# Reordering the first transfers, statistics and transposes at the head of a fused layer-norm, SwiGLU and attention kernel

## The chip, the cores and the metric

One core of one Trainium2 chip. The metric is the device time of one execution in microseconds (us). The kernel before takes 921.5 us. The change touches only the first 13 us.

## The reference

Everything is bf16. x has 2048 tokens (rows) of 640 values. It is layer-normed. The normed rows feed two branches: 32 heads of attention over a cached window of 512 keys, and a SwiGLU feed-forward with 1536 hidden units. The output is x plus the product of both.

```python
xn = _layernorm(x, axis=-1)                       # (x - mean) / sqrt(var + 1e-5)
s = _A_ref(xn, A_k_cache, A_v_cache, A_wq, A_wo)  # windowed attention, then @ wo
g = _silu((_silu(xn @ w_gate) * (xn @ w_up)) @ w_down)
return x + s * g
```

## The kernel before

It begins with the feed-forward of the first 512 tokens, as four token tiles of 128 rows. For each tile: load x, statistics on VectorE (two halves and an aggregation), square root on ScalarE, reciprocal and apply on VectorE, five transposes on TensorE (with 128 x 128 pieces), copies back to SBUF, and then 30 matmuls of 128 columns with the first quarters of the gate and up weights. Each quarter's load is cut in two: a first piece (rows 0 to 255, 192 KB) and a rest (rows 256 to 639, 288 KB). In the traces TensorE, VectorE and ScalarE each start their instructions in the order of the calls, even where a later one could run: in order_alone below, VectorE idles 1.65 us ahead of one call while the data of the next is there. So the place of a call in this code is its place in the queue.

```python
        load_x(0, (nc.scalar, nc.sync))         # half of tile 0 from each queue
        load_x(1, (nc.scalar,))
        load_first(slice(0, 2))                 # first gate piece, first up piece: SyncE's queue
        load_first(slice(2, NC), (nc.sync, nc.scalar))   # gate rest: SyncE, up rest: ScalarE
        nc.scalar.activation(act_t[:], one_t[:], ACT.Sqrt)   # loads the table early
        load_x(2)
        load_x(3)
        load_gu(1)
        # ... further loads
        keep_warm(9)                            # dummy matmuls of 512 columns
        keep_warm(6, P)                         # and of 128 columns

        def ln_stats(t, between=None):
            # ...
            for g in range(ng):                 # ng = 2 halves
                nc.vector.bn_stats(stats[:, g, :], x_t[t][:, g * (D // ng) : (g + 1) * (D // ng)])
                if g == 0 and between:
                    between()
            nc.vector.bn_aggr(ln[b][0][:, ti, :], stats[:])

        def ready(t):                           # transposes, then copies to xnT
            # ... five nc.tensor.transpose into two PSUM tiles
            for tp, cs in zip(tps, PARTS):
                part = tp[:, 0 : cs.stop - cs.start, :]
                if t == 3 and cs.stop == NC:
                    nc.vector.tensor_copy(out=xnT[:, cs, rows], in_=part)
                else:
                    nc.scalar.copy(xnT[:, cs, rows], part)

        ln_stats(0)
        ln_sqrt(0)
        ln_stats(1, lambda: ln_apply(0, (slice(0, 2 * P), slice(2 * P, D))))
        ready(0)
        ln_sqrt(1)
        # ... tile 0: 12 matmuls of the first pieces, then 9 of the gate rest, 9 of the up rest
            for k, (f, s, cs) in enumerate(order):
                if k == len(order) * 4 // 5 and t < 3:
                    if t == 1:
                        ln_stats(3, lambda: ln_apply(2))
                    else:
                        ln_apply(t + 1)
                    ready(t + 1)
                    if t == 0:
                        ln_stats(2)
                    if t < 2:
                        ln_sqrt(t + 2)
                    else:
                        nc.scalar.activation(act_t[:], one_t[:], ACT.Silu)
                hidden_mm(first[f][s][:, rows], s, f, rows, cs)
```

The softmax here doesn't subtract the row's maximum and nothing guards it: scores larger than these inputs give would overflow.

## Time and profile before

| | before |
|---|---|
| time, median of 3 runs | 921.5 us (920.9 to 921.61) |
| span in the profiled run | 919.0 us |
| TensorE busy | 912.8 us (99%) |
| first matmul on real data | 6.26 us |
| token tiles 1, 2, 3 start at | 8.82, 10.89, 12.96 us |

The timelines below have, in this order: start and duration in us, engine, source line, operation, what is written from what, shapes, count; in square brackets the engine's idle time before and what ended it. The transfer lines have size in KB and us from issue to landing.

### The profile page before, as it was taken

Reading aid. Unit: us, or ns where it says so; the run is one execution under the profiler, and the core shown is the slowest. Engines: PE = TensorE matmul, PEld = TensorE weight load, DVE = VectorE, ACT = ScalarE, POOL = GpSimd, SP = SyncE. Lnnn points to the kernel's source line nnn. Section 1 sums busy time; section 2 is a strip of 40 time slices with the busy share of each in tenths; the row PEclk is TensorE's granted clock in tenths of the full one; section 3 lists DMA queues with packets and bytes.
Section 4 is the critical chain, followed back from the end, with each engine's and each line's share of the span. In section 5 each row is a group of like instructions: output and inputs, shape, how many; then the busy total and the mean of one; then the engine's idle time right before and its main releaser. Section 6 shows DMA issues by size and latency. Waiting matters only on the chain.

```text
span 919.0 us, 23151 instructions
## 1 busy us (share of the span) xinstructions
PE 912.8 (99%) x9898; PEld 548.4 (60%) x9920; DVE 601.6 (65%) x844; ACT 474.4 (52%) x840; POOL 85.5 (9%) x269
## 2 busy tenths in 40 slices
PE   9999999999999999999999999999999999999998
PEld 5444444465757575756565656566666666665565
DVE  6443421467677777777777777676867777777657
ACT  4222222557464646565656565655555555556471
POOL 0000000000000000000000000000000000002976
PEclk9999999999999999999999999999999999999999
DMA  9312430045353534253534343435343444343525
GB/s 306 73 35 64 92 81 1 1 75 112 54 113 50 112 49 109 53 108 54 108 58 109 57 109 55 108 52 96 69 84 76 89 78 80 86 71 102 121 58 166
DMA packets 248166, 77.53 MB, mean 84 GB/s; under 512 B 228992, under 2 KB 248064, under 8 KB 248064
## 3 DMA queue, kind: packets, MB, share of 16 engines
q1 hardware_dynamic: 245712, 73.46, 38.6%
q10 hardware_dynamic: 2352, 2.61, 0.8%
q8 instruction: 77, 1.26, 0.6%
q14 instruction: 25, 0.20, 0.1%
HBM read 38.93 MB, written 2.62 MB: 45 GB/s over the span
## 4 chain that ended last, share of the span: by engine, by line
PE 99%; DMA 1%; SPq 0%; issue 0%; DVE 0%
PE mm L450 22%; PE sc L464 18%; PE mm L489 16%; PE sc L604 15%; PE sc L282 11%; PE mm L312 6%; PE sc L574 4%; PE sc L566 2%; PE mm L541 2%; PE mm L566 1%; DMA wg_sb<-in_B_w_gate_dram 1%; PE gu L282 0%; PE mm L321 0%; PE sc L541 0%; PE sc L489 0%
## 5 line engine op out<-in xcount | busy, mean ns | idle before, releaser
L468 ACT ACTIVATE p_t<-sc 128x1024 bf16<-128x1024 f32 x254 | 253.0, 1023 | 120.3 <-PE sc L464 120.3
L455 DVE TENSOR_REDUCE qT<-mm 128x512 bf16<-128x1024 f32 x189 | 231.1, 1223 | 99.1 <-PE mm L450 96.6
L519 ACT ACTIVATE O_b<-mm,r 128x192 bf16<-128x192 f32 x486 | 165.0, 422 | 183.3 <-issue 139.7
L450 PE MATMUL mm<-xnT,wq_p 64*128 64x512 bf16 x1890 | 237.5, 376 | 0.0
L464 PE MATMUL sc<-qT,khat 64*128 64x512 bf16 x1524 | 198.0, 376 | 0.0
L489 PEld LDWEIGHTS <-p_t 64*128 64x128 bf16 x3584 | 159.3, 93 | 33.8
L489 PE MATMUL mm<-V_p,p_t 64*128 64x193 bf16 x3520 | 176.7, 242 | 0.0
L617 DVE TENSOR_TENSOR s_m<-s_m,sc 128x1024 f32<-128x1024 f32 x108 | 131.9, 1221 | 61.1 <-PE sc L604 52.8
L604 PE MATMUL sc<-wo_p,OT_b 64*128 64x512 bf16 x1296 | 168.8, 376 | 0.0
L450 PEld LDWEIGHTS <-wq_p 64*128 64x128 bf16 x1890 | 105.0, 94 | 98.9 <-issue 0.8
L464 PEld LDWEIGHTS <-khat 64*128 64x128 bf16 x1536 | 85.3, 94 | 80.4 <-DVE s_t L617 0.3
L604 PEld LDWEIGHTS <-OT_b 64*128 64x128 bf16 x1296 | 70.0, 94 | 44.2 <-issue 0.3
L617 DVE TENSOR_TENSOR s_t<-s_t,sc 128x512 f32<-128x512 f32 x108 | 74.1, 686 | 28.5 <-PE sc L574 26.6
L591 POOL MEMSET turn_t<- 128x1 f32 x220 | 21.8, 99 | 700.0 <-PE mm L489 506.0
L290 DVE TENSOR_TENSOR hT<-sc,sg 128x512 bf16<-128x512 f32 x46 | 31.7, 691 | 81.6 <-ACT sg L289 81.6
L289 ACT ACTIVATE sg<-sc 128x512 bf16<-128x512 f32 x46 | 27.3, 597 | 69.8 <-PE sc L282 65.1
L282 PE MATMUL sc<-xnT,wg_sb 128*128 128x512 bf16 (+1 forms) x255 | 60.0, 354 | 0.6
L282 PE MATMUL sc<-xnT,wu_sb 128*128 128x512 bf16 (+1 forms) x255 | 59.3, 354 | 0.2
L574 PE MATMUL sc<-OT_b,wo_p 64*128 64x512 bf16 (+1 forms) x345 | 50.3, 376 | 0.0
L312 PE MATMUL mm<-wd_sb,hT 128*128 128x512 bf16 x189 | 43.6, 379 | 0.2
L282 PEld LDWEIGHTS <-wu_sb 128*128 128x128 bf16 x285 | 27.1, 98 | 27.2 <-DMA wu_sb<-in_B_w_up_dram 0.5
L282 PEld LDWEIGHTS <-wg_sb 128*128 128x128 bf16 x285 | 27.0, 98 | 26.6 <-DMA wg_sb<-in_B_w_gate_dram 0.2
(83 smaller groups left out, 417.1 us busy)
## 6 DMA issues: line engine op xcount, KB each, us to landing
wo_p<-in_A_wo_dram SPq DMA_DIRECT2D x16, 480.0 KB, 4.8
K_p<-in_A_k_cache_dram SPq DMA_DIRECT2D x32, 192.0 KB, 4.5
V_p<-in_A_v_cache_dram SPq DMA_DIRECT2D x32, 192.0 KB, 3.3
wq_p<-in_A_wq_dram SPq DMA_DIRECT2D x64, 80.0 KB, 3.0
wq_p<-in_A_wq_dram SPq DMA_DIRECT2D x16, 160.0 KB, 3.3
x_t<-in_A_x_dram SPq DMA_DIRECT2D x14, 160.0 KB, 3.0
x_b<-in_A_x_dram SPq DMA_DIRECT2D x4, 512.0 KB, 5.9
OT_b<-O_b SPq DMA_TRANSPOSE x124, 2.8
```

Of the source, the lines that this page charges most:

```text
L282: nc.tensor.matmul(out, w_sb[:, c, f * P : (f + 1) * P], xnT[:, c, qc], start=(c == 0), stop=(c == NC - 1),)
L290: nc.vector.tensor_tensor(hTs[b][:, f, :], u, sg[:], ALU.mult)
L312: nc.tensor.matmul(dn, at, by, start=(f == 0), stop=(f == NF - 1))
L450: nc.tensor.matmul(q_ps[:, h, :], pairs[pr]["wq"][r, c, j * P : (j + 1) * P], xnT[r, c, b * 512 : (b + 1) * 512], start=(c == 0), stop=(c ...
L455: nc.vector.reduce_sum(qTs[i][:, j, :], q_ps[:, :, :].rearrange("p h n -> p n h"), axis=AX.X)
L464: nc.tensor.matmul(sc[:, h, :], khat[r, j, ks], qT[r, j, :], start=(j == 0), stop=(j == 2))
L468: nc.scalar.activation(p_t[:, :, :], sc[:, :, :], ACT.Exp, scale=scale)
L489: m = nc.tensor.matmul(acc[:, k, h * 256 : h * 256 + Dh + 1], Ps[i][kc][r, h, qt * P : (qt + 1) * P], V_p[r, kc, h, 0 : Dh + 1], start=(p ...
L519: nc.scalar.activation(O_b[:, qt, h, :], a_k[:, h, 0:Dh], ACT.Copy, scale=r[:, k, h, :])
L574: nc.tensor.matmul(ps.rearrange("p (t q) -> p t q", q=P), pairs[i // NB]["wo"][r, j, MC:D], OTs[i][:, :, :].rearrange("p (t j) q -> p j t ...
L604: m = nc.tensor.matmul(ps[:, k, :], OTs[i][r, 3 * (2 * half + k) + j, :], pairs[i // NB]["wo"][r, j, MAIN], start=(turn == 0 and j == 0), ...
L617: nc.vector.tensor_tensor(to, to, ps, ALU.add)
```

## The change

Its intent: get the pieces of weights in the order in which they are used, take a wait out of VectorE by giving it the first half of the next statistics while a square root is under way, and transpose the next tile early enough that ScalarE's copies are done when its matmuls come.

```diff
         load_x(1, (nc.scalar,))
-        load_first(slice(0, 2))
-        load_first(slice(2, NC), (nc.sync, nc.scalar))
+        load_first(slice(0, 2), (nc.sync, nc.scalar))
+        load_first(slice(2, NC))
+        load_x(2, (nc.scalar,))
         nc.scalar.activation(act_t[:], one_t[:], ACT.Sqrt)
-        load_x(2)
         load_x(3)
@@ ready(t)
                 part = tp[:, 0 : cs.stop - cs.start, :]
+                if cs.stop == NC and 1 <= t < 3:
+                    ln_sqrt(t + 1)
@@ the loop over a tile's matmuls
-                if k == len(order) * 4 // 5 and t < 3:
-                    if t == 1:
-                        ln_stats(3, lambda: ln_apply(2))
+                if k == len(order) * 7 // 10 and t < 3:
+                    if t < 2:
+                        ln_stats(t + 2, lambda: ln_apply(t + 1))
                     else:
                         ln_apply(t + 1)
                     ready(t + 1)
-                    if t == 0:
-                        ln_stats(2)
-                    if t < 2:
-                        ln_sqrt(t + 2)
-                    else:
+                    if t == 2:
                         nc.scalar.activation(act_t[:], one_t[:], ACT.Silu)
```

## The prediction

> **What bounds the kernel now.** I read the page's busy shares and its chain first, then what TensorE's weight loads waited for over the whole run, then the timelines of TensorE, VectorE, ScalarE and the transfers of the first 15 us, which is all the change touches. From the page:
>
> ```profile
> PE 912.8 (99%) x9898; PEld 548.4 (60%) x9920; DVE 601.6 (65%) x844; ACT 474.4 (52%) x840; POOL 85.5 (9%) x269
> ...
> PE 99%; DMA 1%; SPq 0%; issue 0%; DVE 0%
> ```
>
> TensorE is busy 912.8 of 919.0 us and is the chain. All that is off TensorE in the chain is the start, up to the landing of one weight piece at 7.36 us. So the change can only win idle time of TensorE in the prologue, and what it wins there should move the rest of the run forward unchanged. The timeline of TensorE, start and duration in us, shows that idle time:
>
> ```profile
> 6.26 0.22 PE L282 MATMUL sc<-xnT,wg_sb 128*128 128x128 bf16 x1
> 6.54 0.23 PE L282 MATMUL sc<-xnT,wu_sb 128*128 128x128 bf16 x1
> ...
> 7.11 0.22 PE L282 MATMUL gu<-xnT,wu_sb 128*128 128x128 bf16 x1
> 7.41 0.28 PE L282 MATMUL sc<-xnT,wg_sb 128*128 128x128 bf16 x2
> ...
> 8.09 0.44 PE L335 MATMUL tp<-ident,xn 128*128 128x128 bf16 x5
> ...
> 8.64 0.22 PE L282 MATMUL gu<-xnT,wu_sb 128*128 128x128 bf16 x1
> 8.82 0.22 PE L282 MATMUL sc<-xnT,wg_sb 128*128 128x128 bf16 x1
> ```
>
> Matmuls of 128 columns follow each other every 0.0555 us (6.61, 6.66, 6.72 and so on). Against that step there are five holes: 6.54 - 6.26 - 0.055 = 0.23 us (the first up-weight piece lands at 6.54); 7.41 - 7.11 - 0.055 = 0.24 us (the rest of the gate piece lands at 7.36); 8.82 - 8.64 - 0.055 = 0.12 us before token tile 1, and the same 0.12 before tile 2 (10.89) and tile 3 (12.96). The last three are the way from the transposes (8.09) over ScalarE's copy to the next matmul: transposes come after 24 of a tile's 30 matmuls, so 6 x 0.055 = 0.33 us is left to cover what takes 0.45. The stretch from 6.26 to 12.96 has this account:
>
> ```profile
> 6.26:12.96 6.70, 6.55 (x105) 5.95 (x105) 4.28 (x14) 2.89 (x10) 0.00 (x0) 1.00 1.09 339
> ```
>
> 105 matmuls and transposes at 0.0555 us are 5.83 us of 6.70: **0.87 us of holes is the whole prize**. The clock (1.00) is full. The column before the last (1.09) says that the transfer engines are saturated, at 339 GB/s.
>
> The transfers, from the transfer views of narrow windows (KB, us from issue to landing):
>
> ```profile
> wu_sb<-in_B_w_up_dram ACTq DMA_DIRECT2D x1, 288.0 KB, 3.9
> ...
> wu_sb<-in_B_w_up_dram SPq DMA_DIRECT2D x1, 192.0 KB, 4.3
> ...
> wg_sb<-in_B_w_gate_dram SPq DMA_DIRECT2D x1, 288.0 KB, 4.6
> ```
>
> Issued at 1.95, 2.24 and 2.74, they landed at 5.85, 6.54 and 7.36. Tile 2 of x, issued behind them at 3.25, landed at 7.84, when VectorE's statistics started. So the piece that is used last landed first. VectorE and ScalarE:
>
> ```profile
> 6.18 0.21 DVE L246 BATCH_NORM_AGGREGATE mv<-stats 128x2 f32<-128x12 f32 x1
> 6.88 0.16 DVE L265 RECIPROCAL rstd<-rstd 128x1 f32<-128x1 f32 x1 [0.50 <-ACT rstd L256]
> 7.08 0.45 DVE L267 TENSOR_SCALAR xn<-x_t,mv,rstd 128x640 bf16<-128x640 bf16 x1
> 7.84 0.89 DVE L243 BATCH_NORM_STATS2 stats<-x_t 128x6 f32<-128x320 bf16 x2 [0.31 <-DMA x_t<-in_A_x_dram]
> ...
> 2.43 1.28 ACT L208 ACT_TABLE_LOAD   x1 [2.43 <-issue]
> 3.72 0.20 ACT L208 ACTIVATE act_t<-one_t 128x1 f32<-128x1 f32 x1
> 4.58 0.29 ACT L256 ACTIVATE rstd<-mv,eps_t 128x1 f32<-128x1 f32 x1 [0.66 <-DVE mv L246]
> ```
>
> VectorE idles 0.50 us waiting for the square root and 0.31 us for x tile 2. ScalarE idles 0.66 us before its first real square root.
>
> **What the Trainium skill says.** "DMA: Bandwidth & Descriptors", section "Issuing engines are not separate DMA queues": transfers of all issuing engines run on the same 16 engines and interleave; issuing from several saves only issue time. The trace agrees: 1.09 share while both queues work, and no faster than with one. So the move to ScalarE's queue buys order, not bandwidth. Same page, "Queues, rings and completion order": each engine takes turns between the queues packet by packet; in the trace ScalarE's queue moved 624 packets by about 5.2 us, beside some 480 of the other. "ScalarE: Activation LUTs", "What ACT_TABLE_LOAD costs": about 1283 ns and a drain of 1380 ns; the trace shows the 1.28 us, but the next activation follows at once (3.72), so I leave the drain out. Same page, "Table sets: the hidden batching unit": copy is in every set, so a square root between two copies needs no load; the trace has copies and square roots in turn from 5.83 to 12.54 with no load between.
>
> **The change, part by part.**
> 1. Queues. ScalarE's queue carries half of x0, x1, first up piece (192 KB), x2 (160 KB); before, the 288 KB up rest stood there. In packets that is 64 + 128 + 256 + 128 = 576, against 64 + 128 + 384 = 576 before (the view counts 16 more for each transfer): the queue ends about as it did. First up piece: it follows x1 (landed 1.30 + 2.6 = 3.9) at the rate of the up rest, 288 KB in 1.95 us, so 192 KB land by about 5.2, before the 6.26 at which TensorE wants them: **the 0.23 hole goes**. x2 behind it, 160 KB more at that rate, about 6.2.
> 2. The rest pieces on SyncE's queue. Up rest now ends with the same bytes delivered (x0, x1, x2 and all four pieces, 1440 KB) as x2 before, so it lands at about 7.84. The gate rest is 288 KB less; that size took 7.36 - 6.54 = 0.82 us behind the first up piece, mostly with the queue alone, so it lands at about 7.02. TensorE wants it at 6.26 + 12 x 0.0555 = 6.93: **0.24 of hole becomes about 0.10**.
> 3. Transposes after 21 of 30. In tile 0 that is exactly between the 9 gate matmuls (7.03 to 7.53) and the 9 up matmuls. The five transposes take 0.28 us, to about 7.83, and bridge the wait for the up rest: **about 0.07 of new hole**. Left behind the transposes are 9 x 0.055 = 0.50 us instead of 0.33, more than the 0.45 the copy needs: **the three holes of 0.12 go, 0.36 us**.
> 4. Can VectorE deliver the applied tile 1 by 7.53? The first half of x2's statistics (0.44 us) moves into the idle 0.50 us between 6.39 and 6.88, since x2 is there by 6.2. Then reciprocal at 6.88, apply 7.08 to 7.53, as before: just in time. The second half and aggregation end at about 8.2; the square root of tile 2 runs between ScalarE's two copies (copy 7.87 to 8.24, root to 8.5, copy to 8.85). The second copy is wanted by 8.37 + 12 x 0.0555 = 9.04. Fits, by 0.2. For tile 1, statistics of x3 from 8.2, reciprocal 8.7, apply to 9.35, wanted at 9.5.
> 5. Table load. x2's issue on ScalarE costs about 0.45 to 0.6 us (its others: 0.45 to 0.60), so the load runs from 2.9-3.0 to 4.3 and the dummy to 4.5; the root is wanted at 4.58. Hidden, by about 0.1.
>
> Sum: holes 0.87 before, 0.10 + 0.07 after, 0.70 us won; tile 3 starts at about 12.26 instead of 12.96. From there TensorE's row is continuous (its weight loads wait under 3 us after the start), so all of it should reach the end. The three times of before have the mean 921.34 and the median 921.5; 921.4 - 0.7 = **920.7 us**.
>
> **Rivals.** (a) x2 lands late. If it comes after 6.4, the in-order VectorE holds apply of tile 1 back, where before it ran first; every 0.1 us goes straight into the transposes, which now stand 0.17 us earlier in TensorE's order. A landing at 7.0 would cost 0.6 and eat nearly all: 921.3. For it: saturation. Against it: the packet count. (b) The up rest becomes the bound, since x2 now goes ahead of it: at 8.3 rather than 7.84, gain 0.25, 921.1. For it: it was the first to land and is now the last. Against it: equal bytes landed by 7.84 before. (c) The later table load pushes the first square root and with it everything by 0.1 to 0.2: 920.9. (d) The early gain is given back later, because some later stage waits for a transfer that did not move: 921.4. Against it: after the prologue the weight loads show waits for transfers of 0.2 us only.
>
> **Range and chances.** Full success in every hole would be 921.4 - 0.87 = 920.5, failure as in (a) 921.3; the three runs of before spread over 0.7 us by themselves. I take 920.0 to 921.5. Two per cent is 18 us, twenty times the prize: within 2% at 0.98, 0.01 on either side.
>
> **What would show it right or wrong.** Right: the first up matmul 0.055 us after the first gate matmul at 6.26; x2's first statistics start at about 6.4, without a wait for the transfer; the five transposes stand between the gate and up matmuls of tile 0 at about 7.55; tiles start at 8.4, 10.3 and 12.3; no hole ahead of tiles 2 and 3. Wrong: a wait of TensorE for the applied tile (rival a), a wait for the up weights over 0.2 us (b), a first matmul after 6.3 (c), or tile 3 at 12.3 with a span that is not shorter (d).

## The result, and the profile after

The changed kernel took 921.09 us (median of 6 runs, 920.45 to 921.48), before 921.56 us (6 runs, 920.9 to 922.18): ratio 0.9994, 95% interval 0.9981 to 1.0007. A ratio is the mean time of one kernel's fast runs over that of the other's of the same rounds, so not quite the ratio of the medians. The time lies inside the predicted range and within 2%, as predicted. But the profiled run shows next to nothing of the working: its span is 919.1 us, against 919.0 before. The page of the changed kernel:

```profile
span 919.1 us, 23174 instructions
...
PE 914.2 (99%) x9920; PEld 548.9 (60%) x9920; DVE 601.8 (65%) x844; ACT 473.9 (52%) x840; POOL 85.2 (9%) x269
```

TensorE's timeline of the changed kernel:

```profile
6.72 0.27 PE L282 MATMUL sc<-xnT,wg_sb 128*128 128x128 bf16 x1
6.78 0.31 PE L282 MATMUL sc<-xnT,wu_sb 128*128 128x128 bf16 x1
6.88 0.31 PE L282 MATMUL sc<-xnT,wg_sb 128*128 128x128 bf16 x1
...
8.06 0.22 PE L282 MATMUL gu<-xnT,wg_sb 128*128 128x128 bf16 x1
8.34 0.45 PE L335 MATMUL tp<-ident,xn 128*128 128x128 bf16 x5
8.63 0.28 PE L282 MATMUL sc<-xnT,wu_sb 128*128 128x128 bf16 x2
...
9.13 0.22 PE L282 MATMUL sc<-xnT,wg_sb 128*128 128x128 bf16 x1
...
11.08 0.22 PE L282 MATMUL sc<-xnT,wg_sb 128*128 128x128 bf16 x1
```

Four things are to be seen. The first matmul comes at 6.72, not 6.26. The first matmuls stand 0.107 us apart, not 0.0555. The hole of 8.34 - 8.06 - 0.055 = 0.22 us lies ahead of the transposes. And the holes before tiles 1 to 3 are gone: tile 1 follows 0.06 us after the last matmul of tile 0 (9.07), and tiles 1, 2 and 3 (9.13, 11.08, 13.04) are 1.955 us apart, against 2.07 before. VectorE and ScalarE in the same run:

```profile
4.87 0.49 DVE L243 BATCH_NORM_STATS2 stats<-x_t 128x6 f32<-128x320 bf16 x1 [0.29 <-DMA x_t<-in_A_x_dram]
...
7.24 0.49 DVE L243 BATCH_NORM_STATS2 stats<-x_t 128x6 f32<-128x320 bf16 x1 [0.50 <-DMA x_t<-in_A_x_dram]
7.65 0.15 DVE L265 RECIPROCAL rstd<-rstd 128x1 f32<-128x1 f32 x1
7.83 0.45 DVE L267 TENSOR_SCALAR xn<-x_t,mv,rstd 128x640 bf16<-128x640 bf16 x1
...
2.95 1.28 ACT L209 ACT_TABLE_LOAD   x1 [2.95 <-issue]
4.24 0.20 ACT L209 ACTIVATE act_t<-one_t 128x1 f32<-128x1 f32 x1
4.61 0.29 ACT L256 ACTIVATE rstd<-mv,eps_t 128x1 f32<-128x1 f32 x1 [0.16 <-DVE mv L246]
```

The wait for x2 (7.24) stands where the prediction's rival (a) put it: ahead of apply of tile 1, which therefore ends at 8.28 and not at 7.53. x1 came late as well (4.87), and since apply of tile 0 stands behind the first half of x1's statistics, the first transposes were late with it. ScalarE's later table load is hidden as predicted: the root starts at 4.61, and it waited 0.16 us for VectorE, not for the table. The transfers, issued at 2.24, 2.75 and 2.43:

```profile
wg_sb<-in_B_w_gate_dram SPq DMA_DIRECT2D x1, 288.0 KB, 5.1
wu_sb<-in_B_w_up_dram SPq DMA_DIRECT2D x1, 288.0 KB, 5.5
x_t<-in_A_x_dram ACTq DMA_DIRECT2D x1, 160.0 KB, 4.8
```

They landed at about 7.3, 8.25 and 7.2 us. Predicted were 7.02, 7.84 and 6.2.

### The profile page after: what moved, and what is told of

Same layout as the page of the kernel before. It is cut to its first block, busy times and chain, and to the rows that moved or that the text cites. A ratio compares the mean times of both kernels' runs of the same rounds, so it can differ in the third digit from the quotient of the medians.

```text
span 919.1 us, 23174 instructions
## 1 busy us (share of the span) xinstructions
PE 914.2 (99%) x9920; PEld 548.9 (60%) x9920; DVE 601.8 (65%) x844; ACT 473.9 (52%) x840; POOL 85.2 (9%) x269
## 4 chain that ended last, share of the span: by engine, by line
PE 99%; DMA 1%; DVE 0%; ACTq 0%; issue 0%
PE mm L448 22%; PE sc L462 18%; PE mm L487 16%; PE sc L602 15%; PE sc L282 11%; PE mm L312 6%; PE sc L572 4%; PE sc L564 2%; PE mm L539 2%; PE mm L564 1%; DMA x_t<-in_A_x_dram 1%; PE gu L282 0%; PE mm L321 0%; PE sc L487 0%; PE sc L539 0%; PE mm L462 0%
```

## The experiments

Twelve kernels ran, in three sets of four, each set on one chip beside the kernel before, five rounds each; all results were accepted as correct. "Mean difference" is the mean of the kernel's fast runs less that of before in the same set; I left out three runs over 923 us (two of before, one of order_alone), which were 2 to 3 us longer at a granted clock of 0.998. One such difference has a standard error of about 0.2 us (0.1 to 0.4). The ratios are as the comparison gave them, all runs in; every interval contains 1. "Span difference" is the same difference taken of the spans, which the record has for every timed run, to 0.1 us, but not for before in the first set; its standard error is 0.12 to 0.25 us. The last four columns are from each kernel's one profiled run.

| kernel | median us | before, median us | ratio | mean difference us | span difference us | first matmul | transposes of tile 1 | tile 3 starts | span |
|---|---|---|---|---|---|---|---|---|---|
| before (first profile) | 921.5 | | | | | 6.26 | 8.09 | 12.96 | 919.0 |
| changed (first set) | 921.09 | 921.56 | 0.9994 | -0.56 | | 6.72 | 8.34 | 13.04 | 919.1 |
| before_again | 921.32 | 921.25 | 0.9996 | +0.12 | -0.10 | 6.57 | 8.19 | 13.07 | 919.1 |
| after_again | 921.10 | 921.25 | 0.9993 | -0.09 | -0.14 | 6.56 | 8.41 | 13.11 | 919.2 |
| queues_alone | 921.53 | 921.25 | 0.9999 | +0.50 | +0.40 | 6.36 | 9.41 | 14.29 | 920.4 |
| order_alone | 921.81 | 921.25 | 1.0004 | +0.57 | +0.48 | 6.28 | 9.15 | 13.86 | 919.9 |
| x2_freed | 921.02 | 921.18 | 0.9996 | -0.36 | -0.36 | 6.54 | 7.79 | 12.59 | 918.7 |
| x1_x2_freed | 920.83 | 921.18 | 0.9996 | -0.37 | -0.28 | 6.30 | 8.26 | 13.00 | 919.1 |
| at70_alone | 921.09 | 921.18 | 0.9998 | -0.15 | 0.00 | 6.23 | 8.11 | 13.01 | 919.0 |
| x2_sync_between | 920.89 | 921.18 | 0.9994 | -0.48 | -0.34 | 6.67 | 8.32 | 13.02 | 919.1 |
| x2_taken_away | 920.87 | 921.39 | 0.9997 | -0.27 | -0.68 | 6.62 | 7.95 | 12.65 | 918.7 |
| after_third | 921.36 | 921.39 | 1.0000 | -0.02 | -0.06 | 6.57 | 8.22 | 12.92 | 919.0 |
| between_freed | 921.25 | 921.39 | 0.9996 | -0.32 | -0.24 | 6.56 | 7.87 | 12.75 | 918.9 |
| fewer_dummies | 920.42 | 921.39 | 0.9991 | -0.86 | -0.58 | 6.22 | 7.55 | 12.69 | 918.8 |

The last two columns hold the firmest finding: span less start of tile 3 is 905.99 to 906.15 us in all fourteen profiles. What happens before 13 us reaches the end unchanged, so the start of tile 3 is a finer measure of these kernels than the time, and the span of a run tells about when its tile 3 started. The time contains something more: it exceeds the span by 1.7 to 2.8 us, and by 3.3 and 3.4 us in two runs of x2_taken_away; the record doesn't show what that is. By the spans, tile 3 at the forecast 12.26 us would be a span of about 918.3; the change's sixteen runs have 918.7 to 920.0, so none of them got there.

### Nothing changed, twice more the change: before_again, after_again, after_third

No edit.

> The kernel before, unchanged, as the null. Both theories: ratio 1.000 within 0.0005. Theory T1 (the gain is real and the profiled run of the changed kernel was an unlucky one, with x tile 1 landing at 4.87 us instead of 3.9 and TensorE still at half clock until 7.2): a second profile of before may itself show another landing of x tile 1 and another moment at which matmuls speed up, and span minus start of token tile 3 stays at 906.04 us to within 0.1, so that all of the spread lies in the prologue. Rival T2 (x1 is late because of the new queue order): x1 lands at 3.9 here again, first matmul at 6.26, tile 3 at 12.96.

> The changed kernel, unchanged. T1: x1 lands near 3.9, first matmul near 6.3, x2 lands before 6.5, tile 3 starts near 12.3, median 0.5 to 0.7 us under before. T2: x1 lands near 4.8 again, first matmul near 6.7, x2 near 7.2, tile 3 near 13.0; median 0 to 0.3 us under before. Both: no hole before tiles 2 and 3, period 1.95 us a tile instead of 2.07.

> The changed kernel a third time, to size the gain: two sets gave means of 0.56 and 0.08 us under before. Theory A: 0.1 to 0.5 us under before, x2 landing at 7.0 to 7.4 us and tile 3 near 13.0 in the profile. The forecast's 0.7 would need x2 by 6.4 and tile 3 at 12.3.

The rival "x1 is late because of the new order" falls as a rule: in after_again and after_third x1's statistics start at 4.50 and 4.49, as early as before_again's 4.56. A late x1 shows only in two profiles, both with the first up piece behind it on ScalarE's queue (4.87, and 4.88 in x2_taken_away); whether that is chance is not shown. x2, in turn, is late in all three profiles of the change: its statistics start at 7.24, 7.31 and 7.13. From the timelines of TensorE and VectorE in after_again:

```profile
8.41 0.45 PE L335 MATMUL tp<-ident,xn 128*128 128x128 bf16 x5 [0.40 <-DVE xn L267]
...
7.31 0.49 DVE L243 BATCH_NORM_STATS2 stats<-x_t 128x6 f32<-128x320 bf16 x1 [0.88 <-DMA x_t<-in_A_x_dram]
```

TensorE had finished the gate matmuls at 7.80 and waited for tile 1 until 8.41.

The null run taught something else. The kernel before itself started its matmuls at 6.57 this time:

```profile
4.62 1.27 PE L230 MATMUL gu<-zero_t 128*128 128x512 bf16 x7
5.68 0.74 PE L335 MATMUL tp<-ident,xn 128*128 128x128 bf16 x5
6.57 0.27 PE L282 MATMUL sc<-xnT,wg_sb 128*128 128x128 bf16 x1
6.62 0.31 PE L282 MATMUL sc<-xnT,wu_sb 128*128 128x128 bf16 x1
6.73 0.31 PE L282 MATMUL sc<-xnT,wg_sb 128*128 128x128 bf16 x1
```

The last dummies (0.107 us apart) held the transposes up until 5.68, and the matmuls kept that half pace until 7.16. In the first profile of before TensorE was at full pace by 5.2, and the transposes started at 5.51. Of the 0.31 us between the two first matmuls, 0.09 are VectorE's apply (5.20 for 5.11), 0.08 the wait behind the dummies (the transposes otherwise start 0.40 us after apply does), and 0.14 the way from the transposes to the first matmul at half pace (0.89 for 0.75).

The Trainium skill explains this: "TensorE: Matmul & The Clock Gate", section "What's actually happening", says that the array runs at half clock until an activity window of about 3.4 us has been busy, and that the window is free-running, so the moment of the step varies from run to run. The runs agree in that it varies: by the distances of the single matmuls the step came at 4.7 us in the earliest of the fourteen profiles (at70_alone), at 7.2 in the latest three, and in the others anywhere between. The section puts the variation at 500 ns either way; here it is 2.5 us from end to end.

In the thirteen profiles with all six short dummies, seven had the dummies still at half pace to the end; their first matmul came at 6.54 to 6.72. In the other six it came at 6.23 to 6.36, but for one with a late x1 (x2_taken_away, 6.62). All three profiles of the change fell in the slow kind, by chance or not; one of the four with the old queue order did. Whether the queue order has a part in it stays open. The granted clock in the profile's views, 1.00 in these stretches, doesn't show this step.

As to time: the three sets give the change 0.56, 0.09 and 0.02 us under before. Its 16 runs have the mean 921.17, all 38 of before (before_again's five among them, the two slow ones left out) 921.36, so 0.20 us, with a standard error of 0.12. That is under a third of the 0.7 us in the forecast and hardly told from nothing. The spans say the same: 919.17 in the mean against 919.33 for before's 32, so 0.16 us, with an error of 0.10.

### Each half alone: queues_alone, order_alone

```diff
 # queues_alone: before, with the change's first hunk only
+        load_first(slice(0, 2), (nc.sync, nc.scalar))
+        load_first(slice(2, NC))
+        load_x(2, (nc.scalar,))
 # order_alone: the change, with before's order of loads (load_x(2) back behind the Sqrt call)
+        load_first(slice(0, 2))
+        load_first(slice(2, NC), (nc.sync, nc.scalar))
```

> Before with the new queue order alone. Both: the hole of 0.23 us for the first up piece goes and that of 0.24 for the gate rest shrinks to 0.1, but the up rest now lands last (8.2 to 8.3 us in the profile of the change), wanted at 7.5, so up to 0.5 us of new hole before the up matmuls of tile 0, as transposes stand after 3 of them. Three holes of 0.12 stay. T1: 0 to 0.2 us faster. T2 (new order delays x1): 0.3 us slower.

> The change without its queue part: x2 on the old queue lands at 7.84 us, and VectorE's first half of its statistics stands ahead of apply of tile 1. Both: apply of tile 1 ends near 8.9 instead of 7.5, TensorE waits about 0.5 us or more for it, tile 0's hole grows; the three holes of 0.12 go. Net 0.2 us slower to 0.2 faster than before. If instead it is as fast as the whole change, the new queue order is worth nothing.

Each alone is worse: half a microsecond slower by the means, and 0.8 to 1.3 us later at tile 3 in the profile. For order_alone this is clear of noise (0.57 with an error of 0.10), for queues_alone just so (0.50 with 0.23). In queues_alone both rests landed late in its one profile (gate rest 2.24 + 5.9, up rest 2.75 + 6.5), and that profile is of the slowest of its five runs (span 920.4, the others 919.2 to 920.2). Its waits, us in total, times, longest:

```profile
PEld L282 <- DMA wg_sb<-in_B_w_gate_dram: 1.2, 1, 1.2
PEld L282 <- DMA wu_sb<-in_B_w_up_dram: 0.5, 1, 0.5
```

I had expected 0.5 us of new hole from the up rest and little from the gate rest; it is the gate rest that cost most. The loads stand in the same order as in the change, where the gate rest landed 0.6 to 0.8 us earlier; why it was so late here is not shown. In order_alone the dependency itself is bare, here on TensorE and VectorE:

```profile
9.15 0.45 PE L335 MATMUL tp<-ident,xn 128*128 128x128 bf16 x5 [0.85 <-DVE xn L267]
...
8.06 0.50 DVE L243 BATCH_NORM_STATS2 stats<-x_t 128x6 f32<-128x320 bf16 x1 [1.65 <-DMA x_t<-in_A_x_dram]
```

VectorE stands 1.65 us idle for x2, with tile 1 loaded and its square root done, because x2's statistics are next in its order. So the shifted statistics are harmful without an earlier x2; that the new queue order is harmful without the rest of the change is seen in the times, but not explained.

### The transposes alone: at70_alone

```diff
-                if k == len(order) * 4 // 5 and t < 3:
+                if k == len(order) * 7 // 10 and t < 3:
```

> Before, with the transposes moved from 24 to 21 of 30 matmuls and nothing else. Theory A: three holes of 0.12 us turn into waits for apply: tile 2's applied values come at 10.03 in before and are wanted at 9.9, tile 3's at 12.1 and wanted at 11.9; so tile 3 starts 12.8 to 12.96, 0 to 0.2 us faster than before. If the holes simply go, 0.36 us faster (tile 3 at 12.6), and the shifted statistics are worth nothing.

Tile 3 at 13.01 and a mean 0.15 us under before: no gain that can be told from none. Tile 1's transposes were at 8.11, tile 2's at 10.21 and tile 3's at 12.22, with 0.6 us of waits for apply in all. So the holes before tiles 2 and 3 turn into waits for VectorE. The one before tile 1 did go (its first matmul follows the last of tile 0 at 8.83 by 0.06 us), but in this run the gate rest landed 0.2 us later than in before and cost more than that. The earlier transposes alone show no gain, as expected.

### Taking x2 out of the way: x2_freed, x1_x2_freed, x2_taken_away

```diff
 # x2_freed: the change, with
-                if cs.stop == NC and 1 <= t < 3:
+                if cs.stop == NC and t == 2:
                     ln_sqrt(t + 1)          # and ln_sqrt(2) after tile 1's copies
-                    if t < 2:
+                    if t == 0:
+                        ln_apply(1)
+                        ln_stats(2)
+                    elif t == 1:
                         ln_stats(t + 2, lambda: ln_apply(t + 1))
 # x1_x2_freed: moreover
-        ln_stats(1, lambda: ln_apply(0, (slice(0, 2 * P), slice(2 * P, D))))
+        ln_apply(0, (slice(0, 2 * P), slice(2 * P, D)))
+        ln_stats(1)
 # x2_taken_away: the change, without load_x(2, (nc.scalar,)); load_x(2) after load_gu(2);
 # statistics and apply of tile 2 read x_t[1] (wrong on purpose)
```

> The change, but in tile 0 VectorE applies tile 1 before any statistics of x2 (and the square root of tile 2 comes after both copies, as its statistics now end later). Theory A (the change loses its gain because apply of tile 1 stands behind the first half of x2's statistics and x2 lands at 7.24 to 7.31 us, not 6.2): the transposes of tile 1 no longer wait 0.4 to 0.6 us for VectorE, they start near 7.7 instead of 8.34 to 8.41, some 0.1 to 0.3 of it turns into a wait for the up rest (landing 8.05 to 8.27), tile 3 starts near 12.7; 0.2 to 0.5 us faster than the changed kernel, 0.4 to 0.7 faster than before. Rival B (the up rest, landing last, bounds tile 0 anyway): tile 3 at 13.0, no gain.

> As x2_freed, and VectorE applies tile 0 before any statistics of x1. Theory C (a late x1 also costs): in the profile of the changed kernel x1 landed at 4.87 us and the first matmul came at 6.72, in three others x1 by 4.5 and the first matmul at 6.26 to 6.57. If such late landings are common, first matmul near 6.2 always, and 0.1 to 0.3 us under x2_freed in the mean; if rare, the same as x2_freed within 0.1, since apply of tile 0 waits for its square root until 4.9 either way.

> A wrong result on purpose: the change, but tile 2's statistics and apply read x tile 1, and x2's own load stands behind the second weight quarters, so x2 (160 KB) is neither waited for nor ahead of the up rest. Theory A (the late x2 and the saturated transfers ate the forecast's gain; the rest of its working holds): no wait of VectorE in tile 0, transposes near 7.5 to 7.7, up rest lands near 7.4 to 7.8, tile 3 starts 12.2 to 12.5, span 918.2 to 918.6, median 0.6 to 0.9 us under before. Rival D (the working is wrong elsewhere: first matmul, copies, clock): tile 3 at 12.9 or later, no better than the changed kernel.

x2_freed does in its profile what theory A says. TensorE's timeline:

```profile
7.68 0.22 PE L282 MATMUL gu<-xnT,wg_sb 128*128 128x128 bf16 x1
7.79 0.45 PE L335 MATMUL tp<-ident,xn 128*128 128x128 bf16 x5
8.08 0.28 PE L282 MATMUL sc<-xnT,wu_sb 128*128 128x128 bf16 x2
```

The transposes follow 0.11 us after the gate matmuls, there is no wait for the up rest, and tile 3 starts at 12.59, though the matmuls began only at 6.54. That is 0.33 to 0.52 us ahead of the three profiles of the change. The times are 0.36 us under before, which is 0.16 better than the change's pooled 0.20, less than its own error.

x2_taken_away, which neither waits for x2 nor sends it ahead, comes to 12.65 although x1 landed at 4.88 there: without VectorE's wait for x2, tile 1's transposes start at 7.95. It was accepted as correct, presumably because what it gets wrong is small beside x, but it is no kernel to use. Its expected start of 12.2 to 12.5 was not reached, because its first matmul came at 6.62: from there to tile 3 it took 6.03 us (x2_freed 6.05), where the forecast had 12.26 - 6.26 = 6.00 and the change took 6.32 to 6.55.

Its times scatter from 920.28 to 922.12, so their mean (-0.27) decides nothing, but its spans do: 918.5 to 918.8, all below the lowest of before's 32 (918.9), and 0.68 us under before in the mean of its set, with an error of 0.12. So without x2 the change wins what was forecast for it, and x2 is what it loses the gain to. This kernel takes away the wait and 160 KB of early transfer at once; x2_freed, which takes away the wait alone, has spans 0.36 us under before, with an error of 0.13. How the loss divides between the two is therefore only roughly known.

x1_x2_freed is a miss that teaches: with both waits taken out, tile 3 starts at 13.00. In its profile the first up piece came at 6.75 (1.95 + 4.8), and the gate rest at 7.75, and TensorE waited for both; the up rest landed at about 8.45, just ahead of its use at 8.54. So the order on VectorE removes only one bound; the landings of the weights are the next, and they vary much between runs. In the six profiles that load in the change's order (the three of the change, x2_freed, x1_x2_freed, queues_alone) the gate rest landed at 7.1 to 8.1, the up rest at 8.05 to 9.25, and x2 at 6.8 to 8.4 us. By the mean it is not better than x2_freed, so a late x1 is rare or cheap.

### Where x2 rides: x2_sync_between, between_freed

```diff
 # x2_sync_between: the change, with
-        load_first(slice(2, NC))
-        load_x(2, (nc.scalar,))
+        load_first(slice(2, NC), (nc.sync,))    # gate rest
+        load_x(2)
+        load_first_up(slice(2, NC))             # up rest, on SyncE's queue
 # between_freed: both this and x2_freed
```

> The change, with x2 on SyncE's queue between the gate rest and the up rest, instead of on ScalarE's. Theory A1 (what decides is how many bytes go ahead of x2 in both queues together, 1152 KB with itself, as saturated engines share): x2 lands near 7.0 to 7.3 here too, same time as the changed kernel within 0.2 us. Rival A2 (ScalarE's queue itself holds x2 up, as it got only some 55 of 180 packets per half us from 5.0 to 6.5): x2 lands earlier, by 6.8, and the kernel is 0.3 us faster than the changed one.

> x2 on SyncE's queue between gate rest and up rest, and apply of tile 1 ahead of x2's statistics. Theory A: the weight pieces land as in x2_sync_between (gate rest 6.8, up rest 7.7 to 8.0), no wait for VectorE; tile 3 near 12.6; 0.4 to 0.7 us under before and the best of these kernels. If the weight pieces decide (rival B), the same as x2_sync_between within 0.1.

x2 lands at about 7.2 on SyncE's queue too (2.75 + 4.5, statistics start at 7.22), and at 7.35 in between_freed and fewer_dummies:

```profile
7.22 0.50 DVE L248 BATCH_NORM_STATS2 stats<-x_t 128x6 f32<-128x320 bf16 x1 [0.52 <-DMA x_t<-in_A_x_dram]
```

So A2 falls, and A1 stands: what x2 waits for is the 1152 KB that go ahead of it and with it, on whichever queue. They give its landing only roughly, as the 6.8 to 8.4 us above are for the same bytes. How the queues shared is shown by the transfer view from 5.0 to 6.5 us (packets, MB, share of 16 engines), first before, then the change; q10 is ScalarE's queue:

```profile
q1 hardware_dynamic: 601, 0.46, 95.2%
q10 hardware_dynamic: 28, 0.02, 3.8%
```

```profile
q1 hardware_dynamic: 398, 0.30, 61.4%
q10 hardware_dynamic: 169, 0.17, 35.4%
```

Before, ScalarE's queue is all but done at 5.0. In the change it isn't, although it holds no more packets: with the end of the first up piece and x2 on it, it gets 30% of the packets (28% and 31% in after_again and after_third). I had carried over the rate of an earlier stretch (288 KB in 1.95 us) to x2.

The rates differ as well. From 4 to 6 us the engines moved 314, 343, 336 and 333 GB/s in the four profiles with the old order, 334, 319 and 337 in the three with x2 on SyncE's queue, but 304, 284, 284, 285, 301 and 299 in the six with x2 on ScalarE's. Between the first and the last of these groups lie some 39 GB/s over 2 us, 77 KB, or 0.2 us of everything behind. But x2_taken_away, with no x2 there at all, moved 304 too, so that it is x2's place is not settled, and nothing that I ran shows why. The times of x2_sync_between are the best of its set (-0.48), those of between_freed don't repeat that (-0.32), and neither is told apart from x2_freed; by the spans the three are within 0.12 us of each other.

### Fewer dummies: fewer_dummies

```diff
 # between_freed, with
-        keep_warm(6, P)
+        keep_warm(2, P)
```

> between_freed with 2 instead of 6 short dummy matmuls ahead of the first transposes. In profiles where TensorE is still at half speed after 5.2 us (matmuls of 128 columns 0.105 us apart instead of 0.0555) the dummies end at 5.7 to 5.9 and hold the first transposes up by 0.2 to 0.3 us. Theory E (that is a part of the spread): transposes at 5.5 in every run, 0.1 to 0.2 us under between_freed. Rival: the clock steps up later for want of work, no gain or 0.2 us slower.

This beats both kernels in the means: 920.42 us median (920.36 to 921.06) against 921.39 for before; four of its five runs lie below the lowest of before's nine (920.8). The interval of its ratio, 0.9978 to 1.0004, still just contains 1, and by the times it is the best of twelve kernels, with five runs, so part of its lead may be luck. TensorE's timeline:

```profile
5.48 0.63 PE L340 MATMUL tp<-ident,xn 128*128 128x128 bf16 x5 [0.17 <-DVE xn L272]
6.22 0.22 PE L287 MATMUL sc<-xnT,wg_sb 128*128 128x128 bf16 x1
...
7.55 0.45 PE L340 MATMUL tp<-ident,xn 128*128 128x128 bf16 x5
8.27 0.29 PE L287 MATMUL sc<-xnT,wu_sb 128*128 128x128 bf16 x2 [0.27 <-DMA wu_sb<-in_B_w_up_dram]
```

TensorE now waits for VectorE ahead of the transposes (0.17) rather than the transposes for the dummies, the first matmul is at 6.22, and the bound has gone back to a transfer: the up rest, landing at 8.27. Its profile fell in a run at full pace, so the saving in a half-pace run is inferred from the times alone. Against between_freed it is 0.55 us, with an error of 0.29, or 0.34 with 0.27 by the spans. That is more than the 0.1 to 0.2 us by which the dummies held the transposes up in the half-pace profiles, and its own profile puts tile 3 at 12.69, against 12.75 and, in x2_freed, 12.59. So it is not shown that the dummies are what it gains by; dropping them from before or from the change alone was not tried.

## Why the prediction was right or wrong

**The time** was right: 920.7 forecast, 921.09 measured in the first set, within the range, and a change of no weight against 2%. That is no merit of the working: the range of 920.0 to 921.5 also takes in the failure of rival (a) and almost no change at all. **The account of the gain** was not right: 0.70 us forecast, 0.20 +- 0.12 over all runs.

**That nothing but the prologue counts, and that its gain is not given back** (rival d): right in all fourteen profiles.

**Step 3, the three holes before the tiles** (0.36 us): right. They are gone; the spacing of tiles fell from 2.07 to 1.955 us. at70_alone shows that tiles 2 and 3 need the shifted statistics for it.

**Step 1, the first up piece and x2**: the piece landed at 5.95 to 6.25 (1.95 + 4.0 to 4.3), where 5.2 was forecast; that was just in time, and the hole of 0.23 is gone. "x2 behind it, 160 KB more at that rate, about 6.2" is the step that failed: 7.13 to 7.31 in three profiles. The rate was measured where ScalarE's queue got most of the packets (in before 363 of 480 from 3.9 to 5.0 us); beside the pieces on SyncE's queue it got 28 to 31% from 5.0 to 6.5. The share of 1.09, which the prediction gives for "while both queues work", is of 6.26 to 12.96 us, when ScalarE's queue was done; from 3.9 to 5.0 us, with both at work, it was 0.97.

**Step 4, VectorE in time for tile 1 at 7.53**: failed with it. Rival (a) had the right mechanism and named the reason for it, saturation; I gave more weight to a count of packets. x2 at 7.2 put apply's end at 8.17 to 8.36. What that cost TensorE was 0.11 to 0.55 us, less where the matmuls had started late themselves. x2_taken_away shows that the rest of the working holds: 6.03 us from the first matmul to tile 3, for 6.00, and spans 0.68 us under before, for 0.70. (Its up rest, without x2 ahead of it, landed at 2.75 + 4.9 = 7.65, so it does not test step 2.)

**Step 2, the rests**: the way was right, the sizes were low by 0.2 to 0.6: gate rest about 7.3 to 7.5 (forecast 7.02), up rest 8.05 to 8.45 (7.84). So rival (b) was right about the landing (8.3). In the change the transposes, late themselves, bridge the wait for the up rest; it comes out where they are early (0.27 us in fewer_dummies).

**Step 5, the table load**: right, the root starts at 4.61, 0.03 later. Rival (c) is out.

**What no step had**: that the first matmul at 6.26 is not the only case of this kernel. In a half-pace run it is 6.57 without any change. By then most of what the change has to win is already landed: in before_again the two holes for weights are mostly filled by the late start itself. So the prize of 0.87 us was read from a run of the kind in which it is largest. Both this and the wait for x2 are shown in traces. How the timed runs divide between the kinds is not known, as only one execution of each kernel has a trace; but the 0.68 us of x2_taken_away leave this second cause little room in the mean.

## What to carry to other kernels

An instruction moved forward in an in-order queue to fill an idle gap brings its own wait along: place it ahead of the critical one only if its data is there with a margin, and read that margin from the bytes ahead of it on all queues together, not from the rate of one queue in another stretch; even so allow for its spread (here 6.8 to 8.4 us for the same bytes). When the forecast gain is of the size of the run-to-run spread, take a second profile of the unchanged kernel first: here before_again shows that the start itself moves by 0.3 us. And where a time is noisier than the effect, compare the spans of all timed runs: here they decided what the times left open.

## What the Trainium skill lacked or had wrong

- "DMA: Bandwidth & Descriptors", sections "Issuing engines are not separate DMA queues" and "Queues, rings and completion order": that issuing from several engines saves only issue time, with turns taken packet by packet. The runs show that the turns need not come to equal halves: from 5.0 to 6.5 us ScalarE's queue got 169 of 567, 169 of 604 and 179 of 577 packets in the three profiles of the change, and from 3.9 to 5.0 us 363 of 480 in before (whether both queues had work on each of the 16 engines all that time is not shown). The sum was lower in one set of orders, 284 to 304 GB/s from 4 to 6 us in six profiles with x2 on ScalarE's queue, against 314 to 343 in four with the old order (cause not settled). The sections have no rule for either.
- "ScalarE: Activation LUTs", section "What ACT_TABLE_LOAD costs": the 1.28 us are confirmed in every run, the drain of 1380 ns is not seen here: the activation behind the load starts 0.01 us after it (2.95 + 1.28, then 4.24), and a later load starts 0.02 us after the copy ahead of it (12.54 + 0.37, then 12.93, in before).
- "TensorE: Matmul & The Clock Gate", section "What's actually happening": the half pace is confirmed (0.107 and 0.056 us a matmul), and of use; the moment of the step varies more than it says (4.7 to 7.2 us). What it lacks is the trap of warm-up work of fixed length in program order: in seven of thirteen profiles the dummies were at half pace to the end. In five of these they held the first transposes up until 5.68 us, by 0.08 to 0.21; in the other two the transposes waited for a late x anyway. The granted clock in the profile's views read 1.00 all the while.
